# Strided attention's second product with V as the stationary operand, normalised by a ones matmul and Ln/Exp

## The chip, the cores and the metric

The kernel runs on one core of a Trainium2 chip. The metric is the device time of one execution in microseconds (us), lower is better; the median of several executions is given. A profile is one further execution recorded by the hardware profiler. The core has five engines that run their own instruction queues in order: TensorE (PE in the profile, PEld for its weight loads), VectorE (DVE), ScalarE (ACT), GpSimd (POOL) and SyncE (SP), the last used for DMA issue. Matmuls write to PSUM, which VectorE and ScalarE read.

## What is computed

A sparse attention over 8 batches and 8 heads (sequence 576, head dimension 64), followed by a two-layer network with squared relu over the 4608 tokens:

```python
pos = np.arange(S)
rel = pos[:, None] - pos[None, :]
mask_local = (rel >= 0) & (rel < 32)
mask_strided = (rel >= 0) & (pos[None, :] % 32 == pos[:, None] % 32)
masks = np.stack([mask_local if h < H // 2 else mask_strided for h in range(H)])
scores = np.where(masks[None], scale * (q @ k.T), -1e9)      # per batch and head
attn = softmax(scores)
x = (attn @ v).transpose(0, 2, 1, 3).reshape(B * S, H * D)   # 4608 x 512
h = np.maximum(x @ w_in, 0.0)                                # 4608 x 2048
out = (h * h) @ w_out                                        # 4608 x 512, float32
```

Heads 0 to 3 of a batch use the local mask, heads 4 to 7 the strided one. Under the strided mask a query sees only keys of its own residue modulo 32.

## The kernel before

Attention is done in 32 units, four per batch: unit u is batch u // 4 and head pair u % 4. Pairs 0 and 1 are local, 2 and 3 strided. The kernel holds x transposed in four tiles `xt[p]` (128 rows are the two heads' 64 features, 4608 columns are tokens), because the first layer of the network reads x with features on the partitions.

For a strided unit the 576 positions of a head are split into 8 blocks of 72 (`SP_`) positions: 4 residues with their 18 members each. A score block is 72 by 72 and needs a mask that is the same for all blocks.

The steps of a unit, each a function:

- `step_T` (L256): transposes q and k on TensorE, in the first batches only; later they come from transposing DMAs.
- `step_S` (L291): score matmuls (L314), 16 for a strided unit, with keys on the output's partitions, so that the exponentials `e` have keys on partitions and queries in the columns. The exponential runs on ScalarE (L319, four of 288 columns), the mask is a multiply on VectorE (L325). `e` is one of four standing tiles.
- `step_D` (L395): the second product. `e` is the stationary operand and V the moving one; V's tile has a 65th column of ones, so that the sum of a row of `e` comes out beside its products (L412). A strided unit has 16 such matmuls in three parts of 6, 6 and 4 (one PSUM tile each). VectorE takes the reciprocal of the sums (L426) and multiplies (L427) into a tile x with queries on the partitions.
- `step_E` (L430): brings x into `xt`: for local units of batch 2 and later by a transposing DMA, for strided units by 8 transposes on TensorE (L444) and a copy out of PSUM with reordered columns (L452, on ScalarE for units below 12, on VectorE from then on).

Batch 0 goes another way, written out by hand in `first_steps` (L516): `step_N` (L354) multiplies a tile of ones (128 by 64) with `e`, which gives the row sums replicated on 64 partitions (L361); ScalarE takes Ln (L363) and Exp with scale -1 (L364) of them, which is the reciprocal; `step_O` (L366) uses V as the stationary operand and `e` as the moving one (L380), which gives x transposed, and VectorE multiplies the two into `xt` (L391).

The network works on 9 chunks of 512 tokens. A group of the first layer is four 512-wide matmuls (L468) into a `ph` PSUM tile (two buffers), a relu on ScalarE (L474) and a square on VectorE (L475). A group of the second layer is four 512-wide matmuls (L486); every fourth group ends with a copy on ScalarE (L497) and a store. Chunk 2's first layer stands alone; from chunk 3 on groups of chunk c's first layer alternate with groups of chunk c-1's second layer into a single `py` buffer.

The order is static. A planner gives each group of the network a due number: how many attention steps have been emitted before it. Each batch's steps are spread by weight over the groups that precede the chunk which first reads that batch, and end two groups ahead of it. `stream_steps` (L558) writes the order of steps: for each u, S of unit u+1, E of unit u-1, then the parts of D of unit u. `later(n, fn, key)` defers an engine instruction by n groups, and `run_due` at the head of a step emits what its unit still has pending. PSUM tiles `pt` of all steps come from one pool of five (`ps_t`).

Of the kernel before, what the change touches and what calls it, by code (L numbers as in the profile page):

```python
# [8 lines left out]
FP32 = mybir.dt.float32  # L9
BF16 = mybir.dt.bfloat16  # L10
AF = mybir.ActivationFunctionType
ALU = mybir.AluOpType

@with_exitstack
def kernel(
# [9 lines left out]
    nc = tc.nc  # L25
    B, H, S, D = q.shape
# [4 lines left out]
    scale = 1.0 / (D ** 0.5)  # L31
    QL = 96
    NL = S // QL
    NJ = 8
    RH = STRIDE // NJ
    SP_ = RH * NA
# [7 lines left out]
    v_st = ctx.enter_context(tc.tile_pool(name="v_st", bufs=2))  # L44
    small = ctx.enter_context(tc.tile_pool(name="small", bufs=4))
    xl_pool = ctx.enter_context(tc.tile_pool(name="xl_pool", bufs=4))
    x_pool = ctx.enter_context(tc.tile_pool(name="x_pool", bufs=2))
    g_pool = ctx.enter_context(tc.tile_pool(name="g_pool", bufs=2))
    r_pool = ctx.enter_context(tc.tile_pool(name="r_pool", bufs=4))
    y_pool = ctx.enter_context(tc.tile_pool(name="y_pool", bufs=4))  # L50

    PS = bass.MemoryType.PSUM
# [4 lines left out]
    ps_t = ctx.enter_context(tc.tile_pool(name="ps_t", bufs=5, space=PS))  # L57
# [12 lines left out]
    xt = [singles.tile([128, T], BF16, name=f"xt{p}") for p in range(4)]  # L70
# [3 lines left out]
    ones = singles.tile([128, D], BF16)  # L74
# [17 lines left out]
    units = [(b, p) for b in range(B) for p in range(H // 2)]  # L92
    st = {}

    def is_local(u):
        return units[u][1] < H // 4
# [145 lines left out]
    def later(n, fn, key=None):  # L242
        pending.append((clock[0] + n, key, fn))

    def run_due(test):
        due = [x for x in pending if test(x)]
        for x in due:
            pending.remove(x)
        for x in sorted(due, key=lambda x: x[0]):
            x[2]()  # L250
# [5 lines left out]
    def step_T(u, name):  # L256
        s = st[u]
        local = is_local(u)
        n, w = (6, QL) if local else (NJ, SP_)
        src = s[name]  # L260
        if u != 1:
            src = src.rearrange("p j h d -> p (j h d)" if local else "p h c -> p (h c)")
        pt = ps_t.tile([128, S], BF16, name="pt")
        for j in range(n):
            if u == 1:
                for h in range(2):
                    nc.tensor.transpose(pt[64 * h:64 * h + 64, w * j:w * (j + 1)],
                                        src[:, h, D * j:D * (j + 1)], ident[0:w, 0:w])
            else:
                nc.tensor.transpose(pt[:, w * j:w * (j + 1)], src[:, 128 * j:128 * (j + 1)],  # L270
                                    ident[0:w, 0:w])
        if local and name == "k":
            full = kTl[v_slot(u)]
            dst = full[:, 32:32 + S]
        else:
            full = dst = qkT.tile([128, S], BF16, name=f"{name}T")
        if local:
            o = dst.rearrange("c (p j) -> c p j", j=6)
            i = pt.rearrange("c (j p) -> c p j", j=6)
        else:  # L280
            o, i = dst, pt
        if name == "q" and u not in (1, 2, 3):
            nc.scalar.copy(o, i)
        else:
            nc.vector.tensor_copy(o, i)  # L285
        s[name + "T"] = full

    def blk_pos(h, j):
        return NJ * (j % 2) + 4 * h + j // 2
# [64 lines left out]
    def step_N(u):  # L354
# [8 lines left out]
            nc.scalar.activation(rv0[:, u, hw * half:hw * (half + 1)], pn[:, 0:hw], AF.Ln)  # L363
        nc.scalar.activation(rv0[:, u], rv0[:, u], AF.Exp, scale=-1.0)  # L364

    def step_O(u):  # L366
        s = st.pop(u)
        e, local, i = s["e"], is_local(u), u % 2
        kn, w, hw = (128, QL, S // 2) if local else (SP_, SP_, S // 2)
        pos = []  # L370
        for half in range(2):
            po = ps_t.tile([128, 512], FP32, name="pt")
            for t in range(hw // w):
                for h in range(2):
                    if local:
                        tt = NL // 2 * half + t
                        vt, c = vl0[:, i, h, tt], S * h + w * tt
                    else:
                        vt, c = vs0[:, i, NJ * h + 2 * t + half], S * half + hw * h + w * t
                    nc.tensor.matmul(po[64 * h:64 * h + 64, w * t:w * (t + 1)], vt, e[0:kn, c:c + w],  # L380
                                     start=True, stop=True)
            pos.append(po)

        def scaled():
            for half, po in enumerate(pos):
                cols = slice(hw * half, hw * (half + 1))
                o, x, r = xt[u][:, cols], po[:, 0:hw], rv0[:, u, cols]
                if not local:
                    o = xt[u][:, 0:S].rearrange("c (p j r) -> c p j r", j=NJ // 2, r=2)[:, :, :, half]
                    x, r = (y.rearrange("c (j p) -> c p j", p=SP_) for y in (x, r))  # L390
                nc.vector.tensor_tensor(o, x, r, op=ALU.mult)  # L391

        return scaled

    def step_D(u, part):  # L395
        run_due(lambda x: x[1] == u)
        s = st[u]
        e, vt = s["e"], s["v"]
        if is_local(u):
            w, kn, n0, n1, tot = QL, 128, 6 * part, 6 * part + 6, 2 * NL  # L400
            rhs = vt.rearrange("p h t d -> p (h t) d")
            pos = lambda n: QL * n
            src = lambda n: n
        else:
            w, kn, tot = SP_, SP_, NBS
            n0, n1 = ((0, 6), (6, 12), (12, 16))[part]
            rhs = vt
            pos = lambda n: SP_ * blk_pos(n % 2, n // 2)
            src = lambda n: NJ * (n % 2) + n // 2
        po = ps_t.tile([128, 6, D + 1], FP32, name="pt")  # L410
        for n in range(n0, n1):
            nc.tensor.matmul(po[:, n - n0, :], e[0:kn, pos(n):pos(n) + 128],  # L412
                             rhs[0:kn, src(n), 0:D + 1], start=True, stop=True)
        if part == 0:
            if is_local(u):
                s["x"] = xl_pool.tile([w, tot, D], BF16, name="x_l")
            else:
                s["x"] = x_pool.tile([w, tot, D], BF16, name="x_s")
        x = s["x"]
        if is_local(u):  # L420
            x = x.rearrange("p (t h) d -> p h t d", h=2)[:, part]
        else:
            x = x[:, n0:n1, :]
        m = n1 - n0
        rinv = small.tile([128, 6, 1], FP32, name="rinv")
        nc.vector.reciprocal(rinv[0:w, 0:m], po[0:w, 0:m, D:D + 1])  # L426
        nc.vector.tensor_tensor(x, po[0:w, 0:m, 0:D],  # L427
                                rinv[0:w, 0:m].to_broadcast([w, m, D]), op=ALU.mult)
# [71 lines left out]
    T_ = lambda u, nm: (lambda: step_T(u, nm))  # L500
    S_ = lambda u: (lambda: step_S(u))
    D_ = lambda u, part: (lambda: step_D(u, part))
    E_ = lambda u: (lambda: step_E(u))

# [11 lines left out]
    def first_steps():  # L516
# [11 lines left out]
        def outs(u):  # L528
            scaled[u] = step_O(u)
# [25 lines left out]
    def has_T(u):  # L555
        return units[u][0] < (LB if is_local(u) else XB)

    def stream_steps(lo, hi, base):  # L558
        order = [T_(lo, "q"), T_(lo, "k"), T_(lo + 1, "q"), S_(lo), T_(lo + 1, "k")]
        ends = {}  # L560
        for u in range(lo, hi + 1):
            if u < hi - 1:
                order.append(S_(u + 1))
            ahead = u + 2 < hi and has_T(u + 2)
            if ahead:
                order.append(T_(u + 2, "q"))
            if u > lo:
                order.append(E_(u - 1))
                ends[u - 1] = base + len(order)
            if u < hi:  # L570
                order.append(D_(u, 0))
                if ahead:
                    order.append(T_(u + 2, "k"))
                order.append(D_(u, 1))
                if not is_local(u):
                    order.append(D_(u, 2))
        return order, ends
# [95 lines left out]

    NCH = T // 512
    steps, ends = stream_steps(4, 8, 0)
    more, more_ends = stream_steps(8, 4 * B, len(steps))
    steps = steps + more
    ends.update(more_ends)
# [112 lines left out]
```

## Time and profile before

| | us |
|---|---|
| median of 6 runs | 316.88 (316.37 to 318.46) |
| the profiled execution, whole time | 317.12 |
| its span, first to last instruction | 315.1 |
| VectorE busy | 172.0 |
| ScalarE busy | 162.7 |
| POOL busy | 89.0 |
| L468, first layer: 572 matmuls recorded | 145.0 |
| L486, second layer: 576 matmuls | 145.5 |
| L412, second product of attention: 392 matmuls | 22.9 |
| L444, transposes of x: 124 matmuls | 7.4 |

How to read it: a busy time is the union of the recorded durations of an engine's instructions. A matmul's recorded duration contains its way through the array, so consecutive matmuls overlap in the records, and the time that a block of them takes from TensorE is read from the starts. The difference of about 2 us between an execution's whole time and its span lies before the first and after the last instruction.

### The profile page before, as it was taken

The page shows a single profiled execution, that of the slowest core. Times are in us where ns is not written, and L with a number is a line of the kernel's source. Part 1 is how long each engine was busy: PE and PEld are TensorE (multiplying, and loading weights), DVE is VectorE, ACT ScalarE, POOL GpSimd, SP SyncE. Part 2 cuts the span into 40 slices and gives each one's busy share as a digit, 9 for nine tenths or more (in the row PEclk, how much of TensorE's full clock was granted, in tenths as well). Part 3 has the DMA queues.
Part 4 walks back from the last instruction along what each step waited for, and adds up shares of the span by engine and source line. Part 5 has one row for each costly group of instructions (what it writes and reads, how often), then busy time and mean ns, then how long its engine had stood idle before and what let it go on. Part 6 is the DMA issues. An engine that isn't in the chain of part 4 may idle for free.

```text
span 315.1 us, 6213 instructions
## 1 busy us (share of the span) xinstructions
PE 303.8 (96%) x2384; PEld 149.4 (47%) x2384; DVE 172.0 (55%) x415; ACT 162.7 (52%) x337; POOL 89.0 (28%) x117
## 2 busy tenths in 40 slices
PE   8899989899999999999999999999999999999994
PEld 3444555444555444444444444444454444444441
DVE  6765655469876885576479646564454222222200
ACT  3846746477455765555555555555533434344311
POOL 8518843707830704281066025000000000000000
PEclk9969999999999999999999999999999999999999
DMA  8999999999999999999899795002111000000111
GB/s 146 163 207 204 206 188 258 213 257 221 190 163 202 211 200 192 183 247 214 157 229 204 151 207 88 23 30 60 57 47 41 34 35 34 33 35 33 63 70 67
DMA packets 89404, 43.81 MB, mean 139 GB/s; under 512 B 74112, under 2 KB 82976, under 8 KB 89184
## 3 DMA queue, kind: packets, MB, share of 16 engines
q1 hardware_dynamic: 74352, 32.91, 48.6%
q0 software_dynamic: 14880, 10.39, 22.9%
q8 instruction: 18, 0.29, 0.4%
q14 instruction: 10, 0.08, 0.1%
q10 hardware_dynamic: 144, 0.13, 0.1%
HBM read 36.70 MB, written 12.98 MB: 158 GB/s over the span
## 4 chain that ended last, share of the span: by engine, by line
PE 86%; DVE 7%; ACT 3%; DMA 1%; issue 1%; DVEq 0%
PE ph L468 38%; PE py L486 27%; PE ph L486 10%; PE pt L314 3%; PE pt L412 3%; DVE e L325 2%; DVE x_s L427 2%; PE pt L270 2%; PE pt L444 1%; DVE g_sb L475 1%; ACT e L319 1%; DMA q_st<-in_q_dram 1%; ACT r L474 1%; PE py L511 1%; DVE kTl L285 1%
## 5 line engine op out<-in xcount | busy, mean ns | idle before, releaser
L468 PE MATMUL ph<-xt,w_in_b 128*128 128x512 bf16 x572 | 145.0, 382 | 0.3 <-ACT r L474 0.3
L474 ACT ACTIVATE r<-ph 128x512 bf16<-128x512 f32 x143 | 85.3, 597 | 99.8 <-PE ph L468 98.2
L475 DVE TENSOR_TENSOR g_sb<-r 128x512 bf16<-128x512 bf16 x144 | 71.4, 501 | 101.3 <-ACT r L474 100.7
L486 PE MATMUL py<-w_out_b,g_sb 128*128 128x512 bf16 x400 | 102.7, 379 | 0.0
L486 PEld LDWEIGHTS <-g_sb 128*128 128x128 bf16 x576 | 52.7, 98 | 56.5
L468 PEld LDWEIGHTS <-w_in_b 128*128 128x128 bf16 x576 | 52.0, 98 | 55.3 <-issue 2.4
L319 ACT ACTIVATE e<-pt 128x288 bf16<-128x288 f32 (+1 forms) x128 | 47.3, 407 | 12.6 <-PE pt L314 12.4
L486 PE MATMUL ph<-w_out_b,g_sb 128*128 128x512 bf16 x176 | 42.8, 379 | 0.0
L412 PEld LDWEIGHTS <-e 128*128 128x128 bf16 (+1 forms) x392 | 20.8, 97 | 16.0 <-DVE e L325 0.6
L192 POOL CAST vl<-vl_st 128x768 bf16<-128x768 f32 x12 | 11.0, 914 | 53.3 <-DMA vl_st<-in_v_dram 53.1
L427 DVE TENSOR_TENSOR x_s<-pt,rinv 72x384 bf16<-72x384 f32 (+1 forms) x42 | 21.4, 509 | 1.4
L123 POOL CAST q_l<-q_st 96x768 bf16<-96x768 f32 x14 | 12.3, 882 | 25.3 <-DMA q_st<-in_q_dram 16.3
L325 DVE TENSOR_TENSOR e<-e,mask_loc 128x576 bf16<-128x576 bf16 x32 | 17.5, 546 | 2.2 <-ACT e L319 2.2
L325 DVE TENSOR_TENSOR e<-e,mask_str 72x576 bf16<-72x576 bf16 x32 | 17.6, 554 | 1.8 <-ACT e L319 1.8
L426 DVE RECIPROCAL rinv<-pt 96x6 f32<-96x6 f32 (+2 forms) x70 | 12.9, 184 | 8.4 <-PE pt L412 8.4
L497 ACT COPY y<-py 128x512 f32<-128x512 f32 x25 | 14.6, 585 | 4.4 <-PE py L486 4.1
L427 DVE TENSOR_TENSOR x_l<-pt,rinv 96x384 bf16<-96x384 f32 x28 | 15.5, 554 | 1.0
L123 POOL CAST k_l<-k_st 96x768 bf16<-96x768 f32 x14 | 12.7, 910 | 10.9 <-DMA k_st<-in_k_dram 10.7
L497 ACT COPY y<-ph 128x512 f32<-128x512 f32 x10 | 5.8, 585 | 17.4 <-PE ph L486 17.4
L208 POOL CAST vs<-v_st 72x1024 bf16<-72x1024 f32 x12 | 13.1, 1118 | 0.4
L412 PE MATMUL pt<-vs,e 72*128 72x65 bf16 x224 | 13.1, 193 | 0.0
L511 PE MATMUL py<-y 128*128 128x512 bf16 x24 | 9.9, 503 | 1.3 <-DVE y L637 1.3
(87 smaller groups left out, 166.7 us busy)
## 6 DMA issues: line engine op xcount, KB each, us to landing
out_dram<-y SPq DMA_DIRECT2D x35, 256.0 KB, 2.0
vl_st<-in_v_dram SPq DMA_DIRECT2D x24, 144.0 KB, 4.5
v_st<-in_v_dram SPq DMA_DIRECT2D x12, 288.0 KB
q_st<-in_q_dram SPq DMA_DIRECT2D x16, 144.0 KB, 4.7
k_st<-in_k_dram SPq DMA_DIRECT2D x16, 144.0 KB, 6.1
w_in_b<-in_moe_w_in_dram POOLq DMA_DIRECT2D x4, 512.0 KB, 12.6
w_out_b<-in_moe_w_out_dram POOLq DMA_DIRECT2D x4, 512.0 KB, 10.8
q_st<-in_q_dram SPq DMA_DIRECT2D x7, 288.0 KB, 9.9
```

Of the source, the lines that this page charges most:

```text
L123: copy(t.rearrange("p j h d -> p h j d"), s[name + "f"].rearrange("p h (j d) -> p h j d", j=6))
L208: (copy or nc.gpsimd.tensor_copy)(t[:, :, 0:D], s["vf"].rearrange("p h (j d) -> p (h j) d", d=D))
L319: nc.scalar.activation(e[0:kn, lo:lo + S // 2], banks[row][half][0:kn, 0:S // 2], AF.Exp, scale=scale)
L325: nc.vector.tensor_tensor(x, x, m.to_broadcast([kn, n, w]), op=ALU.mult)
L412: nc.tensor.matmul(po[:, n - n0, :], e[0:kn, pos(n):pos(n) + 128], rhs[0:kn, src(n), 0:D + 1], start=True, stop=True)
L427: nc.vector.tensor_tensor(x, po[0:w, 0:m, 0:D], rinv[0:w, 0:m].to_broadcast([w, m, D]), op=ALU.mult)
L468: nc.tensor.matmul(ph, w_in_b[:, kk, 128 * ff:128 * (ff + 1)], xt[kk][:, 512 * c:512 * (c + 1)], start=(kk == order[0]), stop=(kk == order ...
L474: nc.scalar.activation(r, ph, AF.Relu)
L475: later(1, lambda: nc.vector.tensor_tensor(g[:, ff, :], r, r, op=ALU.mult))
L486: nc.tensor.matmul(py, g[:, ff, 128 * j:128 * (j + 1)], w_out_b[:, ff, :], start=(ff == 0), stop=(ff == 15))
L497: nc.scalar.copy(y, py)
L511: nc.tensor.matmul(pw, idle_w[:, 0:128], idle_w[:, 0:512], start=True, stop=True)
```

## The change

From batch 3 on (units 14, 15, 18, 19 and so on to 30, 31: ten units) the strided units no longer run `step_D` and `step_E`. In place of `step_D` they run `step_R`, which does what `step_N` does in batch 0: four ones matmuls of 288 columns, two Ln, one Exp. In place of `step_E` they run `step_Q`, which does what `step_O` does in batch 0: sixteen matmuls with V as the stationary operand, and two multiplies on VectorE straight into `xt`. The second Ln, the Exp and the second multiply are deferred by one, two and one groups. The result of Ln and Exp, 128 by 576 in f32, lies in a new pool `rv_pool` of two buffers, from which the x tiles of the earlier strided units are now cut as well (the pool `x_pool` is gone). Each of these units makes two steps where it made four, so the planner spreads the steps of batches 3 to 7 anew. Local units and batches 0 to 2 keep their steps.

```diff
-    x_pool = ctx.enter_context(tc.tile_pool(name="x_pool", bufs=2))
+    rv_pool = ctx.enter_context(tc.tile_pool(name="rv_pool", bufs=2))
...
+    XO = 3
+
+    def by_cols(u):
+        return not is_local(u) and units[u][0] >= XO
+
+    def step_R(u):
+        run_due(lambda x: x[1] == u)
+        s = st[u]
+        e, hw = s["e"], S // 2
+        s["r"] = r = rv_pool.tile([128, S], FP32, name="rv")
+        for half in range(2):
+            pn = ps_t.tile([128, 512], FP32, name="pt")
+            for h in range(2):
+                c = S * half + hw * h
+                nc.tensor.matmul(pn[64 * h:64 * h + 64, 0:hw], ones[0:SP_], e[0:SP_, c:c + hw],
+                                 start=True, stop=True)
+            ln = lambda half=half, pn=pn: nc.scalar.activation(r[:, hw * half:hw * (half + 1)], pn[:, 0:hw], AF.Ln)
+            if half == 0:
+                ln()
+            else:
+                later(1, ln, u)
+        later(2, lambda: nc.scalar.activation(r, r, AF.Exp, scale=-1.0), u)
+
+    def step_Q(u):
+        run_due(lambda x: x[1] == u)
+        s = st.pop(u)
+        b, p = units[u]
+        e, vt, r, hw = s["e"], s["v"], s["r"], S // 2
+        for half in range(2):
+            po = ps_t.tile([128, 512], FP32, name="pt")
+            for t in range(hw // SP_):
+                for h in range(2):
+                    c = S * half + hw * h + SP_ * t
+                    nc.tensor.matmul(po[64 * h:64 * h + 64, SP_ * t:SP_ * (t + 1)],
+                                     vt[:, NJ * h + 2 * t + half, 0:D], e[0:SP_, c:c + SP_],
+                                     start=True, stop=True)
+            o = (xt[p][:, b * S:(b + 1) * S]
+                 .rearrange("c (p j r) -> c p j r", j=NJ // 2, r=2)[:, :, :, half])
+            mul = lambda o=o, po=po, half=half: nc.vector.tensor_tensor(
+                o, po[:, 0:hw].rearrange("c (j p) -> c p j", p=SP_),
+                r[:, hw * half:hw * (half + 1)].rearrange("c (j p) -> c p j", p=SP_), op=ALU.mult)
+            if half == 0:
+                mul()
+            else:
+                later(1, mul)
...
-                s["x"] = x_pool.tile([w, tot, D], BF16, name="x_s")
+                t = rv_pool.tile([128, S], FP32, name="rv").bitcast(BF16)[0:w, 0:tot * D]
+                s["x"] = t.rearrange("p (n d) -> p n d", d=D)
...
             if u > lo:
-                order.append(E_(u - 1))
+                order.append((lambda u=u - 1: step_Q(u)) if by_cols(u - 1) else E_(u - 1))
                 ends[u - 1] = base + len(order)
-            if u < hi:
+            if u < hi and by_cols(u):
+                order.append(lambda u=u: step_R(u))
+                if ahead:
+                    order.append(T_(u + 2, "k"))
+            elif u < hi:
                 order.append(D_(u, 0))
```

## The prediction, made before the changed kernel was run

> **What bounds the kernel now.** I read the page's busy shares first, then its forty slices, then the waits, and last the timeline of TensorE alone in the stretch that the change touches.
>
> ```profile
> span 315.1 us, 6213 instructions
> ...
> PE 303.8 (96%) x2384; PEld 149.4 (47%) x2384; DVE 172.0 (55%) x415; ACT 162.7 (52%) x337; POOL 89.0 (28%) x117
> ...
> PE   8899989899999999999999999999999999999994
> ...
> PEclk9969999999999999999999999999999999999999
> ```
>
> TensorE is at nine tenths in every slice from the tenth to the end and has its full clock there; VectorE and ScalarE are a little over half busy. One slice is 7.9 us. The strided units of batches 3 to 7 lie between about 98 and 240 us, so inside that solid row.
>
> ```profile
> DVE g_sb L475 <- ACT r L474: 100.7, 111, 3.1
> ACT r L474 <- PE ph L468: 98.2, 123, 4.0
> ```
>
> These are the two longest waits: VectorE waits for ScalarE, and ScalarE for TensorE. Nothing of comparable size waits the other way. Since a busy TensorE need not be a full one, I then read when each block of matmuls starts. Columns of the next two fences: start in us, length, engine, line, instruction, count. A block's price is the distance from its start to the next block's start, because the lengths overlap.
>
> ```profile
> 157.81 0.38 PE L468 MATMUL ph<-xt,w_in_b 128*128 128x512 bf16 x1
> 158.12 0.47 PE L314 MATMUL pt<-qT_s,kT_s 64*72 64x72 bf16 x16
> 158.52 1.04 PE L486 MATMUL py<-w_out_b,g_sb 128*128 128x512 bf16 x4
> 159.40 1.03 PE L468 MATMUL ph<-xt,w_in_b 128*128 128x512 bf16 x4
> 160.26 1.03 PE L486 MATMUL py<-w_out_b,g_sb 128*128 128x512 bf16 x4
> 161.12 0.35 PE L412 MATMUL pt<-vs,e 72*128 72x65 bf16 x6
> 161.31 1.03 PE L468 MATMUL ph<-xt,w_in_b 128*128 128x512 bf16 x4
> ...
> 164.95 0.29 PE L412 MATMUL pt<-vs,e 72*128 72x65 bf16 x4
> 165.07 1.03 PE L468 MATMUL ph<-xt,w_in_b 128*128 128x512 bf16 x4
> ...
> 168.99 0.42 PE L444 MATMUL pt<-ident,x_s 72*128 72x72 bf16 x8
> 169.25 1.03 PE L468 MATMUL ph<-xt,w_in_b 128*128 128x512 bf16 x4
> ```
>
> Every group of four wide matmuls takes 0.86 us (159.40 to 160.26), that is 0.216 each; no gap is left. So in this stretch the end moves by exactly what a block on TensorE gains or loses; time saved on VectorE buys nothing here.
>
> **What the Trainium skill says.** "TensorEngine Tiling (Array Packing)", Key Properties: a change of tiling mode drains the array. The trace agrees: the score block L314, which uses 64-row tiles, makes the wide matmul before it last 0.31 (157.81 to 158.12) or more where 0.216 is normal, and the group behind it takes 0.88 in place of 0.86; L412 and L444, which use the whole array, do neither. The same page, Restrictions, says that column tiling switches Fast Weight Load off: loads of 64 columns for L361 and L380 average 107 to 137 ns in the trace, those of 128 columns for L412 97, so half the columns are not quicker. "ScalarE: Activation LUTs", Table sets, puts Ln and Exp in one set, natural_log_exp_and_others; the trace has a single table load (1.3 us, at the start) although batch 0 runs both, so the new Ln and Exp cost no reload.
>
> **The change, part by part.** It concerns ten units (batches 3 to 7, pairs 2 and 3).
>
> Removed from TensorE, per unit: the three blocks of step D, 161.12 to 161.31 = 0.19, a second six the same 0.19, and four at 164.95 to 165.07 = 0.12; the eight transposes of step E, 168.99 to 169.25 = 0.26. Sum 0.76 us for 24 matmuls. All of it is on the path.
>
> Added to TensorE, per unit: step R, four 288-wide ones matmuls, and step Q, sixteen 72-wide ones with V as weights, both with outputs of 64 partitions, so in column tiles. Batch 0 already runs both shapes for its strided units (72 rows; 12.24 and 15.58 for R, 15.85 for Q), and the windows view gives a granted clock of 1.00 from 7.3 to 17.4 us:
>
> ```profile
> 11.92 0.39 PE L511 MATMUL py<-y 128*128 128x512 bf16 x1
> 12.24 0.44 PE L361 MATMUL ph<-e,ones 72*64 72x288 bf16 x4
> 12.61 0.39 PE L511 MATMUL py<-y 128*128 128x512 bf16 x1
> ...
> 15.26 0.39 PE L511 MATMUL py<-y 128*128 128x512 bf16 x1
> 15.58 0.44 PE L361 MATMUL ph<-e,ones 72*64 72x288 bf16 x4
> 15.85 0.43 PE L380 MATMUL pt<-e,g_sb 72*64 72x72 bf16 x16
> 16.21 0.39 PE L511 MATMUL py<-y 128*128 128x512 bf16 x1
> ```
>
> R between two full-array blocks: 12.24 to 12.61 = 0.37, and the wide matmul ahead of it takes 0.32 (11.92 to 12.24) where 0.216 is normal: 0.10 more. With R followed by another block of the same mode it is 0.27 (15.58 to 15.85), so leaving the mode costs another 0.10, which is already in the 0.37. Q, left for the full array: 15.85 to 16.21 = 0.36, exit included; entered from the full array it pays the same 0.10 as R. To each I add the 0.01 to 0.02 that the group behind L314 loses (taken 0.01). In the changed program's instruction order every one of the ten R and ten Q stands alone between groups of full-array matmuls, never next to the other or to a score block, so each pays both drains: R 0.48, Q 0.47, sum 0.95 us for 20 matmuls. Fewer instructions, but four changes of mode where there were none.
>
> Difference: 0.95 - 0.76 = 0.19 per unit, times ten = +1.9 us. Bounds: readings are to 0.01, some six per unit, and a Q whose weights strided by 72 load a little slower, or whose loads reach ahead a little better: 0.13 to 0.27 per unit, +1.3 to +2.7 us.
>
> VectorE, per unit: gone are three reciprocals (0.19, 0.19, 0.17), three multiplies (0.55, 0.55, 0.42) and the copy L452 (0.75): 2.82. New are two multiplies of 128x288 from PSUM, at L391's mean of 0.54: 1.08. Minus 17 us over ten units, on an engine that waits 100.7 us for ScalarE's relu: worth nothing to the end. The multiplies wait for Q and for R's Exp; behind them in VectorE's queue are the squares L475 and masks L325. Q follows its R by four groups or more and a score block; by three groups for unit 30 and two (1.73 us) for unit 31. Since the two Ln and the Exp, with the relu of one group between, are done about 3.1 us after R's start and unit 31's Q ends at about 2.6, only that multiply waits, some 0.6 us. The last strided unit of a batch has two groups, 1.73 us, before the first matmul that reads its x, against 0.2 + 2 x 0.54 = 1.3 us; that matmul takes this pair's x as its fourth operand, 0.65 later. No stall.
>
> ScalarE, per unit: two Ln of 128x288 (0.41 to 0.43 at L363) and one Exp of 128x576 in f32 (0.68 at L364): 1.5 us, plus 15 over all, to about 178 of 317. Hidden in its 98 us of waiting, if they do not fall in the wrong place. There are two such places. One is the stretch from about 100 to 117 us, where the first-layer groups stand without second-layer groups between: a relu of 0.60 is due every 0.86, with only two ph buffers, and the windows view shows ScalarE busy 13.2 of 18.0 us; both strided units of batch 3 land there and bring 3.0. The order puts R, two groups, scores, two groups, Q, so that TensorE's own small blocks (0.5 each) give the relu time: I take nothing, upper end 0.5 a unit. The other is the copy L497 out of the single py buffer: TensorE needs it back one group (0.86) after the matmuls end, and the copy takes 0.59. In the order of the changed program an Ln stands before such a copy (as an exponential of 0.40 does now, without a stall), an Exp never does. Cost nothing, upper end 0.25 each.
>
> Buffers: R takes two and Q two of the five pt, in place of D's three and E's one; rv has two buffers and R of one unit comes after Q of the one two before. POOL's casts into vs wait for Q instead of D's last block, some groups later, but POOL spends 53.1 us waiting for the v loads. No DMA is added or removed. The steps are spread anew because each of these units now makes two fewer; score blocks of later batches come a little later against their loads, not earlier.
>
> The sum stands against the profiled execution's own 317.12 us (span 315.1 and 2.0 around it): 319.0. That execution lies 0.24 above the median of 316.88, so the forecast for the median is 318.8 us.
>
> **Rivals.** (a) Faster: the drains are not paid. Place: the entry and exit of each R and Q. Were weights and matmuls of the two column halves to flow through, R would cost 0.27 and Q 0.26 (0.36 less its exit), 0.53 against 0.76, and ten units would give -2.3: 314.6. It speaks for it that batch 0's blocks stand among few neighbours in a stretch with short waits; against it that three different wide matmuls ahead of column-tiled blocks take 0.32, and L314 shows the same in the stretch in question. It decides from the point where a change of mode costs under 0.057 us (0.23 over four) in place of 0.105. (b) Slower by more: ScalarE takes TensorE's place in batch 3 and at the y copies: 2 x 0.5 and, say, three of 0.25 on top: 318.8 + 1.7 = 320.5. For it: a relu queue with 0.27 idle per group; against it: the order, as told. (c) No change: VectorE's relief ends small stalls elsewhere. TensorE's stalls on VectorE (L444 and L314 before 90 us) lie in batches 1 and 2, which keep the old path; what could be regained after 98 us is nil. That would need 1 to 2 us: about 317.
>
> **How the numbers follow.** The forecast 0.80, (a) 0.08, (b) 0.09, (c) 0.03. About 0.3% (0.95 us) is what can be told from no change: 315.9 to 317.8. The forecast's own range is 318.2 to 319.6; with its lower tail and part of (b) 317.5 to 320.5. Faster 0.07, same 0.08 (c, and the edges of the forecast and (a)), slower 0.85.
>
> **What would show it.** Right: ones blocks of 0.37 and V blocks of 0.36, start to start, each with a wide matmul of 0.32 ahead; 2344 matmuls; VectorE near 155 us, ScalarE near 178; no gap over 0.15 in TensorE past 100 us. Wrong: R and Q together under 0.76 with their edges (a); TensorE idle on ScalarE's relu or Exp, around 100 to 117 us or behind a y copy (b).

## The result and the profile after

| | before | changed |
|---|---|---|
| median, us | 316.37 (63 runs) | 318.68 (28 runs) |
| profiled execution, whole time and span | 317.12, 315.1 | 318.73, 317.0 |
| VectorE busy | 172.0 | 154.4 |
| ScalarE busy | 162.7 | 174.3 |
| start of unit 14's scores | 93.6 | 92.3 |
| from there to the group behind the last attention block | 146.5 | 149.7 |

The ratio is 1.0074, with a 95% interval from 1.0056 to 1.0093: 2.3 us slower, 1.8 to 2.9. The forecast was 318.8 us. In what follows a ones block is the four matmuls of `step_R` and a V block the sixteen of `step_Q`. Single executions of either kernel spread over 4 us and more, so the experiments below are read from medians with their intervals and, more sharply, from the starts in the traces. Of one run, b0_before_again, only the times are used, since its trace was taken in an execution of 323.18 us at a TensorE clock of 0.948.

The page of the changed kernel, the lines shown of before:

```profile
span 317.0 us, 6118 instructions
...
PE 303.7 (96%) x2344; PEld 144.1 (45%) x2344; DVE 154.4 (49%) x365; ACT 174.3 (55%) x367; POOL 89.5 (28%) x117
...
PE   7889989999999999999999999999999999999994
...
PEclk9979999999999999999999999999999999999999
```

TensorE has 40 matmuls fewer and the same 96%; the digits show nothing of the loss. The longest waits and one new one, from the view of waits (us in total, times, longest):

```profile
DVE g_sb L522 <- ACT r L521: 117.0, 111, 3.0
ACT r L521 <- PE ph L515: 89.0, 113, 2.4
...
PE pt L314 <- DMA kTl<-k_l: 1.2, 1, 1.2
```

VectorE's 17.6 us of relief have gone into its waiting for the relu, 100.7 us before and 117.0 now. The third line is new: TensorE waits for transposed keys. The timeline of TensorE in batch 5 of the changed kernel (start, length, line, instruction, count):

```profile
164.50 1.03 PE L533 MATMUL py<-w_out_b,g_sb 128*128 128x512 bf16 x4
165.37 1.03 PE L515 MATMUL ph<-xt,w_in_b 128*128 128x512 bf16 x4
166.32 0.44 PE L380 MATMUL pt<-e,ones 72*64 72x288 bf16 x4
166.69 1.04 PE L533 MATMUL py<-w_out_b,g_sb 128*128 128x512 bf16 x4
...
170.62 1.03 PE L533 MATMUL py<-w_out_b,g_sb 128*128 128x512 bf16 x4
171.58 0.45 PE L399 MATMUL pt<-e,vs 72*64 72x72 bf16 x16
171.96 1.04 PE L515 MATMUL ph<-xt,w_in_b 128*128 128x512 bf16 x4
172.84 1.03 PE L533 MATMUL py<-w_out_b,g_sb 128*128 128x512 bf16 x4
```

A plain group takes 0.87 (164.50 to 165.37, read to 0.01). The group ahead of the ones block takes 0.95 (165.37 to 166.32) and the one ahead of the V block 0.96; the blocks take 0.37 and 0.38; the group behind takes 0.88. So a unit costs 0.37 + 0.38 + 2 x 0.09 + 2 x 0.01 = 0.95 to 0.96 us where it was 0.75 to 0.76, and ten units 2.0 us.

The weight loads (PEld) show what is missing at a change of mode. The first four lines are of before, the last three of the changed kernel; the brackets hold the loader's idle time and what ended it ("issue": nothing that the profile shows):

```profile
144.06 0.28 PEld L314 LDWEIGHTS <-kTl 64*128 64x128 bf16 x12 [0.42 <-issue]
144.07 0.43 PE L314 MATMUL pt<-kT,kTl 64*128 64x96 bf16 x12
...
145.09 0.51 PEld L444 LDWEIGHTS <-x_s 72*128 72x128 bf16 x8
145.30 0.42 PE L444 MATMUL pt<-ident,x_s 72*128 72x72 bf16 x8
...
108.10 0.14 PEld L380 LDWEIGHTS <-ones 72*64 72x64 bf16 x4 [0.42 <-DVE g_sb L522]
108.10 0.44 PE L380 MATMUL pt<-e,ones 72*64 72x288 bf16 x4
108.46 1.41 PEld L515 LDWEIGHTS <-w_in_b 128*128 128x128 bf16 x8 [0.23 <-issue]
```

The transposes L444 stay in the mode of the full array: their first weights load from 145.09, while the last wide matmul still runs, 0.21 us ahead of their first matmul. At the ones block the loader stands idle for 0.42 us and begins together with the matmuls, and behind the block it is the same: the wide group loads from 108.46 and starts at 108.47. All ten ones blocks show the 0.42 us, whatever is named as releaser. The scores L314 of a local unit show them too, and they load 128 columns of weights, so it is not the 64 columns that keep the load back.

The other part of the trace is one wait in batch 3, in the timeline of all engines (SPq is SyncE's issue of a DMA; in brackets idle time and what ended it):

```profile
105.68 1.33 SPq L173 DMA_TRANSPOSE kTl<-k_l  x1
...
108.10 0.44 PE L380 MATMUL pt<-e,ones 72*64 72x288 bf16 x4
...
108.47 1.90 PE L515 MATMUL ph<-xt,w_in_b 128*128 128x512 bf16 x8
...
111.55 0.43 PE L314 MATMUL pt<-kT,kTl 64*128 64x96 bf16 x12 [1.18 <-DMA kTl<-k_l]
```

The scores of unit 17 (the second local unit of batch 4) wait 1.18 us for keys whose transposing DMA was issued at 105.68. Between the two profiles, then: 1.3 us less up to unit 14's scores, where both kernels run the same steps (TensorE had half its clock there for 6.8 us in before's profile and for 3.4 in the changed kernel's), 2.0 us more for changes of tile mode, and 1.2 us more for this wait; together the 1.9 us between the spans.

### The profile page after: what moved, and what is told of

It is laid out like the page before. It is cut to its first block, busy times and chain, and to the rows that moved or that the text cites. A ratio compares the mean times of both kernels' runs of the same rounds, so it can differ in the third digit from the quotient of the medians.

```text
span 317.0 us, 6118 instructions
## 1 busy us (share of the span) xinstructions
PE 303.7 (96%) x2344; PEld 144.1 (45%) x2344; DVE 154.4 (49%) x365; ACT 174.3 (55%) x367; POOL 89.5 (28%) x117
## 4 chain that ended last, share of the span: by engine, by line
PE 83%; DVE 6%; DMA 5%; POOL 3%; ACT 1%; issue 1%; POOLq 0%; DVEq 0%
PE ph L515 37%; PE py L533 27%; PE ph L533 10%; PE pt L314 3%; DMA g_sb<-in_v_dram 3%; DMA kTl<-k_l 2%; DVE rv L474 2%; PE pt L458 2%; DVE e L325 1%; PE pt L270 1%; PE pt L399 1%; PE pt L380 1%; DVE g_sb L522 1%; ACT r L521 1%; DVE kTl L285 1%
## 5 line engine op out<-in xcount | busy, mean ns | idle before, releaser
L522 DVE TENSOR_TENSOR g_sb<-r 128x512 bf16<-128x512 bf16 x144 | 66.8, 465 | 117.8 <-ACT r L521 117.0
L319 ACT ACTIVATE e<-pt 128x288 bf16<-128x288 f32 (+1 forms) x128 | 48.0, 407 | 11.9 <-PE pt L314 11.8
L325 DVE TENSOR_TENSOR e<-e,mask_str 72x576 bf16<-72x576 bf16 x32 | 18.8, 591 | 7.9 <-ACT e L319 7.8
L325 DVE TENSOR_TENSOR e<-e,mask_loc 128x576 bf16<-128x576 bf16 x32 | 17.5, 547 | 3.7 <-ACT e L319 3.7
L458 PEld LDWEIGHTS <-e 128*128 128x128 bf16 (+1 forms) x232 | 12.0, 97 | 9.1 <-DVE e L325 0.8
L208 POOL CAST vs<-v_st 72x1024 bf16<-72x1024 f32 x12 | 14.1, 1204 | 0.4
L404 DVE TENSOR_TENSOR xt<-pt,rv 128x288 bf16<-128x288 f32 x20 | 12.1, 638 | 0.7 <-ACT rv L387 0.6
L458 PE MATMUL pt<-vl,e 128*128 128x65 bf16 x168 | 9.9, 193 | 0.7 <-DVE e L325 0.7
L473 DVE RECIPROCAL rinv<-pt 96x6 f32<-96x6 f32 (+2 forms) x40 | 7.4, 185 | 6.2 <-PE pt L458 6.2
L558 PE MATMUL py<-y 128*128 128x512 bf16 x24 | 9.0, 462 | 1.3 <-DVE y L688 1.3
```

The costliest lines, as they stand in the source:

```text
L208: (copy or nc.gpsimd.tensor_copy)(t[:, :, 0:D], s["vf"].rearrange("p h (j d) -> p (h j) d", d=D))
L319: nc.scalar.activation(e[0:kn, lo:lo + S // 2], banks[row][half][0:kn, 0:S // 2], AF.Exp, scale=scale)
L325: nc.vector.tensor_tensor(x, x, m.to_broadcast([kn, n, w]), op=ALU.mult)
L404: mul = lambda o=o, po=po, half=half: nc.vector.tensor_tensor(o, po[:, 0:hw].rearrange("c (j p) -> c p j", p=SP_), r[:, hw * half:hw * (ha ...
L522: later(1, lambda: nc.vector.tensor_tensor(g[:, ff, :], r, r, op=ALU.mult))
```

## The experiments

The ratios below are to executions of the kernel before made beside each run (medians 316.07 to 316.29 us). "Drain theory" in the recorded expectations is the prediction's account: each entry into column tiles and each exit from them costs TensorE about 0.1 us.

The sharpest measure is the stretch from the scores of unit 18 to those of unit 31, which holds six of the ten units (batches 4 to 6). The two starts are read from each trace, and 0.863 us for each group of four wide matmuls between them is taken off (in before's trace three groups take 2.59, from 113.74 to 116.33); the rest is what attention costs TensorE there, waits included. The groups are counted from the weight loads. Some traces lack a few per cent of the matmul records; such a place shows as three matmuls where four are issued, with 0.16 us of idle, and is no wait. Each row is one trace.

| run | the two starts, us | groups between | rest, us | entries into column tiles |
|---|---|---|---|---|
| before | 119.38, 222.63 | 104 | 13.5 | 0 |
| changed | 121.50, 228.54 | 107 | 14.7 | 12 |
| e0_after_again | 120.59, 227.63 | 107 | 14.7 | 12 |
| e1_merge_q_r | 123.48, 230.51 | 107 | 14.7, of it 0.7 a wait | 9 |
| e2_split_q | 123.81, 232.20 | 107 | 16.0 | 18 |
| e3_same_spacing | 118.48, 222.93 | 104 | 14.7 | 12 |
| e4_act_load | 118.78, 222.03 | 104 | 13.5 | 0 |
| e5_merge_same_spacing | 120.81, 224.58 | 104 | 14.0 | 9 |
| e7_two_blocks | 118.55, 223.17 | 104 | 14.9, of it 1.5 waits | 6 |

**e0_after_again**: the changed kernel, unedited.

> The changed kernel once more, beside the runs below. The drain theory (ten units, each with two changes into and two out of column tiles, 0.10 us each, against 0.23 us saved on the matmuls themselves) expects 2.0 us more than before, 1.0065, and in the trace 0.37 and 0.38 us for every ones and V block with a wide matmul of about 0.31 ahead. If the wait of unit 17's scores for its transposed keys (1.2 us at 110 us in the first profile) belongs to the change and not to that one execution, it is there again, and part of the loss is the new spacing of the steps.

319.48 us (6 runs), 1.0093 of before (1.0056 to 1.013). The blocks are as in the first profile, the rest is 14.7 again, and the wait of unit 17 is there again with 0.69 us. So the first profile was no exception on either point.

**e2_split_q**: each V block in two halves.

```diff
-        for half in range(2):
+
+        def one(half):
             po = ps_t.tile([128, 512], FP32, name="pt")
...
-            mul = lambda o=o, po=po, half=half: nc.vector.tensor_tensor(
+            nc.vector.tensor_tensor(
...
-            if half == 0:
-                mul()
-            else:
-                later(1, mul)
+
+        one(0)
+        later(1, lambda: one(1))
```

> The V block is cut into its two halves, the second emitted one group of wide matmuls later: same matmuls, ten exits and ten entries more. Drain theory: 10 x 0.2 = 2.0 us more than the changed kernel, 1.013 of before. Rivals (ScalarE's load, spacing of the steps): as the changed kernel, 1.007.

320.04 us, 1.0126 (1.0088 to 1.0164). Its timeline of TensorE:

```profile
180.22 1.03 PE L533 MATMUL py<-w_out_b,g_sb 128*128 128x512 bf16 x4
181.17 0.32 PE L400 MATMUL pt<-e,vs 72*64 72x72 bf16 x8
181.43 1.04 PE L515 MATMUL ph<-xt,w_in_b 128*128 128x512 bf16 x4
182.39 0.32 PE L400 MATMUL pt<-e,vs 72*64 72x72 bf16 x8
182.65 1.04 PE L533 MATMUL py<-w_out_b,g_sb 128*128 128x512 bf16 x4
```

Eight matmuls take 0.26, not half of the sixteen's 0.38, and the groups ahead take 0.95 and 0.96: both halves pay. The rest grew by 1.35 us for six entries more, 0.22 each. The matmuls, their operands and the work of the other engines are the same, so the price is in the change of mode.

**e1_merge_q_r**: the opposite direction, first try: the second unit's ones block straight behind the first unit's V block.

```diff
-                order.append((lambda u=u - 1: step_Q(u)) if by_cols(u - 1) else E_(u - 1))
+                if by_cols(u - 1) and u < hi and by_cols(u):
+                    order.append(lambda u=u: (step_Q(u - 1), step_R(u)))
+                else:
+                    order.append((lambda u=u - 1: step_Q(u)) if by_cols(u - 1) else E_(u - 1))
...
-                order.append(lambda u=u: step_R(u))
+                order.append((lambda: None) if by_cols(u - 1) else (lambda u=u: step_R(u)))
```

> The ones block of the second strided unit of each batch is put straight behind the V block of the first, with an empty step in its old place so that all other steps stay where they were. Same matmuls, five exits from and five entries into column tiles fewer. Drain theory: 5 x 0.2 = 1.0 us less than the changed kernel, 1.003 of before. Rival, ScalarE's new Ln and Exp or the instruction counts hold TensorE up: no difference to the changed kernel, since all of these stay, 1.007. Rival, spacing of the steps: no difference either.

319.34 us, 1.0087 (1.006 to 1.0114): no gain. The trace shows why the median doesn't fall. The merged block comes two groups after a score block and needs PSUM tiles that ScalarE's exponentials have not yet read: the ten ones blocks take 4.9 us, start to start, where they take 3.7 in the changed kernel (the 1.7 us that e5's expectation names come from 5.4, which counts two missing records as time). Two of the five merged blocks wait, 0.7 each, those of batches 3 and 4. And unit 17's wait was 1.89 us in this execution, after which the clock fell; the windows view (window and its length, busy time of PE, PEld, DVE, ACT and POOL with counts, then PEclk, DMA share and GB/s):

```profile
109.90:112.00 2.10, 0.21 (x3) 0.05 (x4) 0.88 (x3) 0.60 (x1) 0.43 (x1) 1.00 1.28 217
112.00:113.40 1.40, 1.40 (x17) 0.74 (x18) 0.00 (x0) 0.42 (x2) 0.00 (x0) 0.99 1.35 295
113.40:116.80 3.40, 3.18 (x23) 1.36 (x23) 2.02 (x5) 1.79 (x4) 0.00 (x0) 0.50 1.06 210
```

TensorE is nearly idle in the first row and has half its clock for the 3.4 us of the third. In the stretch of the table the one merged block that waits loses the 0.7 us that three entries fewer save: 14.7 less 0.7 is 14.0, which e5, without that wait, shows directly.

**e5_merge_same_spacing**: as e3 (below), with the V block moved back to the ones block instead of the reverse, so that it stands three groups or more behind the scores.

```diff
+                pair = by_cols(u - 1) and u < hi and by_cols(u)
+                order.append((lambda: None) if pair else
+                             (lambda u=u - 1: step_Q(u)) if by_cols(u - 1) else E_(u - 1))
...
+                order.extend([(lambda u=u: (step_Q(u - 1), step_R(u))) if by_cols(u - 1)
+                              else (lambda u=u: step_R(u)), lambda: None, lambda: None])
```

> As e3 (two empty steps for each strided unit, score blocks where the kernel before has them), and the V block of the first strided unit of a batch is put straight ahead of the ones block of the second, three groups or more after the scores, so that the PSUM tiles it needs are free. Drain theory: five entries and five exits fewer than e3, 1.0 us less, that is 1.0 us or 1.0032 over before, and in the trace no wait of the ones blocks for ScalarE (in e1 they lost 1.7 us so). Rivals: as e3, 1.0065.

318.34 us (6 runs), 1.0073 (1.0049 to 1.0098): the median alone doesn't show the microsecond. The trace does: the rest is 14.0 where e3 has 14.7, 0.7 us for three entries fewer, 0.23 each, and the ones blocks wait for nothing.

```profile
170.57 1.03 PE L515 MATMUL ph<-xt,w_in_b 128*128 128x512 bf16 x4
171.53 0.45 PE L399 MATMUL pt<-e,vs 72*64 72x72 bf16 x16
171.81 0.41 PE L380 MATMUL pt<-e,ones 72*64 72x288 bf16 x4
```

The V block that is followed by another block of its mode takes 0.28 (171.53 to 171.81) in place of 0.38, and the ones block pays no entry. In this execution unit 17 waited 1.21 us, more than the gain.

**e7_two_blocks**: as e3, with both ones blocks of a batch together and both V blocks together.

```diff
-                order.append((lambda u=u - 1: step_Q(u)) if by_cols(u - 1) else E_(u - 1))
+                order.append((lambda: None) if by_cols(u - 1) else E_(u - 1))
...
-                order.append(lambda u=u: step_R(u))
+                if by_cols(u - 1):
+                    order.extend([lambda u=u: (step_R(u - 1), step_R(u)), lambda: None,
+                                  lambda u=u: (step_Q(u - 1), step_Q(u))])
+                else:
+                    order.extend([lambda: None] * 3)
```

> As e3, but of each batch's two strided units the ones blocks stand together and the V blocks stand together, four groups later: two entries and two exits a batch in place of four (five in e1's manner). The traces so far put one entry with its exit at 0.2 to 0.23 us. Drain theory: between the scores of unit 18 and those of unit 31 TensorE's time outside the wide matmuls falls from 14.68 us (changed kernel) to 13.3 to 13.5, as low as before (13.48); median as before, 1.000 to 1.002. If the price sat in the matmuls themselves it would stay at 14.68.

317.81 us, 1.0047 (1.0024 to 1.007). The blocks came out as expected, the rest did not:

```profile
168.37 1.03 PE L515 MATMUL ph<-xt,w_in_b 128*128 128x512 bf16 x4
169.32 0.68 PE L380 MATMUL pt<-e,ones 72*64 72x288 bf16 x8
169.94 1.04 PE L533 MATMUL py<-w_out_b,g_sb 128*128 128x512 bf16 x4
...
175.97 0.34 PE L314 MATMUL pt<-kT,kTl 64*128 64x96 bf16 x7
176.50 0.28 PE L314 MATMUL pt<-kT,kTl 64*128 64x96 bf16 x5 [0.18 <-DVE xt L404]
```

Two ones blocks in one take 0.62 (169.32 to 169.94), not 2 x 0.37, and pay one entry. But two V blocks hold four of the five `pt` tiles until VectorE's multiplies have read them, and the scores two groups later wait for one: twelve score matmuls take 0.75 (175.97 to 176.72, where the next group starts) in place of 0.36. Over the three batches in the stretch these blocks lose 1.5 us beyond their 0.36. Without that the rest would be 13.4, what the drain theory expected (13.3 to 13.5) and no more than before has; that is a sum, not a run.

**e4_act_load**: the kernel before with ScalarE's load added.

```diff
+    def act_load():
+        one = lambda: nc.scalar.activation(fill, fill, AF.Exp, scale=0.0)
+        one()
+        later(1, one)
+        later(2, one)
+        later(2, one)
...
+        if part == 0 and not is_local(u) and units[u][0] >= 3:
+            act_load()
```

> The kernel before, with four activations of 128x288 added to ScalarE's queue at each strided unit of batches 3 to 7, deferred as the changed kernel's Ln and Exp are (1.6 us a unit; their result is not used). Drain theory: ScalarE has the room, no difference to before, 1.000. Rival, ScalarE's added work holds TensorE up: up to the 2.3 us of the change, 1.003 to 1.007.

317.07 us, 1.0029 (1.0006 to 1.0051). In the stretch of batches 4 to 6 the rest is 13.5, equal to before within a hundredth: ScalarE's added work costs nothing there. The excess sits ahead of it. The trace has TensorE waiting 1.1 us for the key transposes of units 16 and 17 and 0.5 for ScalarE's relu near 100 us, where first-layer groups stand alone. So ScalarE's load doesn't explain the changed kernel's loss in batches 4 to 6; in batch 3 it may add something, which this run does not separate from the transposes.

**e3_same_spacing**: two empty steps behind each ones block, so that the planner counts as before.

```diff
-                order.append(lambda u=u: step_R(u))
+                order.extend([lambda u=u: step_R(u), lambda: None, lambda: None])
```

> Two empty steps stand behind each ones block, so that a strided unit makes as many steps as before and every score block and every batch end is at the group where the kernel before has it. Drain theory: the 2.0 us stay, 1.0065 of before. Rival, the new spacing brings score blocks ahead of their key transposes: the wait of unit 17's scores goes, and 0.3 to 1.2 us of the loss with it, 1.003 to 1.0055.

318.64 us, 1.0077 (1.0049 to 1.0104), the rest 14.7: with the old spacing the mode changes cost what they cost in the new. Unit 17 did not wait in this trace, but the median is not lower than the changed kernel's by anything that can be told.

Is the wait of unit 17 a matter of the spacing? In the new spacing its scores come one group earlier (17 groups behind unit 14's, not 18). TensorE's wait for transposed keys ahead of the scores of units 16 and 17 was 1.18, 0.69, 1.89 and 2.17 us in the four traces with that spacing (changed, e0, e1, e2) and 0, 0.03, 1.08, 1.21, 0.54 and 0 in six with the old one (before, e3, e4, e5, e6, e7). So it can happen in either; in these traces it is in all four of the new and in three of six of the old.

**e8_transposes_earlier, e9_before_transposes_earlier, e10_two_blocks_earlier**: the transposes of local q and k four groups earlier in SyncE's queue, in the changed kernel, in the one before, and in e7.

```diff
-            at(g + 14 + 4 * i, lambda u=4 * b + i: transpose_local(u))
+            at(g + 10 + 4 * i, lambda u=4 * b + i: transpose_local(u))
```

> The changed kernel with the transposing DMAs of the local units' q and k (batches 4 to 7) put four groups earlier into SP's queue, ahead of the v loads. If the wait of unit 17's scores is for a transpose that stands too late in that queue, the stretch from unit 14's to unit 17's scores loses the 0.7 to 1.2 us seen in the two profiles of the changed kernel, and the median falls by as much, to about 1.005. If it is a matter of the score blocks' new places alone, this changes it too; if the DMA engines are simply full then, it stays.

> The kernel before with the same earlier transposes. If the wait belongs to the new spacing alone, nothing to gain, 1.000. If it can happen in the old spacing too (e4 and e5 showed 0.8 and 1.2 us of it), 0 to 0.8 us less than before, 0.9975 to 1.000.

> e7 and e8 together, the version meant to be no worse than before: drain theory and the earlier transposes together give 0.9975 to 1.001 of before. Rivals: as the changed kernel, 1.007.

320.98, 318.24 and 320.32 us; 1.0137 (1.0082 to 1.0191), 1.0065 (1.0043 to 1.0086) and 1.0146 (1.0095 to 1.0197). None of the three traces has a wait for transposed keys. For e8 that tells something, since all four earlier traces with its spacing have one: the place in the queue mattered. All three are slower all the same, by 2.2 to 2.5 us against their like. In e9 the order of instructions on TensorE, VectorE, ScalarE and POOL is that of before, but in batch 2 TensorE now waits for VectorE where it did not:

```profile
84.65 0.35 PE L412 MATMUL pt<-vs,e 72*128 72x65 bf16 x6
...
85.96 0.41 PE L270 MATMUL pt<-ident,k_l 96*128 96x96 bf16 x6 [0.96 <-DVE x_s L427]
...
88.45 0.29 PE L412 MATMUL pt<-vs,e 72*128 72x65 bf16 x4 [0.88 <-DVE x_s L427]
```

The transposes of keys and the last part of the second product wait for tiles that VectorE's multiplies still read; in before the same two follow without such a wait. Most of the loss lies behind this point: e9 and e4 have the same steps up to unit 14's scores and ran at full clock up to there; they are level at this place (84.65 and 84.56 us), and unit 14's scores start at 93.3 in e9, at 91.0 in e4. From unit 18 to 31 e9's rest is 13.6 and e8's 14.7, as without the move. Why a moved DMA brings these waits stayed open; another assignment of PSUM tiles is a guess that no run tested. As a remedy the move failed.

**e6_batches_1_2_only**: the new path where VectorE did hold TensorE up.

```diff
-        return not is_local(u) and units[u][0] >= XO
+        return not is_local(u) and 1 <= units[u][0] < XO
```

> The new path for the strided units of batches 1 and 2 only, the old one from batch 3 on. There the profile of before has TensorE waiting for VectorE's multiplies (about 0.9 us at each of two transposes, 54.9 and 58.3 us). Drain theory: four units x 0.2 = 0.8 us more on TensorE, and these two waits of 0.9 go: 1.0 us less than before, 0.997. Rival, the waits only move to the Ln and Exp, or the relief of VectorE is worth nothing here either: 0.8 us more than before or worse, 1.0025.

318.73 us (6 runs), 1.0107 (1.0068 to 1.0145): slower by 3.4 us, more than the 0.8 us of mode changes. The two waits of transposes on the strided multiplies are gone, but the ones blocks now wait for masks (0.8 us) and score blocks for exponentials (0.9) and for the key copies on VectorE (1.9 in four waits, up to 92 us): the wait moved, as the rival had it. The rest from unit 18 to 31 is 13.5, as it must be.

**b0_before_again**: the kernel before, unedited.

> The kernel before once more, for its trace beside the others of this call: from the first strided scores of batch 3 to the last attention block it should again take 146.5 us with no wait of TensorE, whatever its first 93 us take. If those first 93 us come out 1 to 2 us shorter this time, the difference seen there between the two first profiles is chance; if they come out at 93.6 again, the changed kernel gains something there.

316.38 us, 1.0006 (0.9989 to 1.0024). For the first 93 us the other traces answer: unit 14's scores start at 93.6 (before), 92.3 (changed), 91.9 (e0), 91.0 (e4) and 91.3 (e3), all with the same steps up to there. The changed kernel's 1.3 us there are chance: the time at half clock in the first 25 us was 6.8 us in before's profile, 3.4 in changed and e3, none in e0 and e4. The stretch of 146.5 us could not be compared, since this trace had a lower clock throughout.

No version beat the kernel before. The best of the new path was e7 with 1.0047.

## Why the prediction was right

The direction, the size and the mechanism came out as forecast. That 318.8 us lies within 0.2 of the median is in part luck: the forecast added 1.9 us to a median of 316.88 from six executions, which 63 executions put at 316.37, and the measured difference is 2.3. The 2.3 lies in the forecast's range of +1.3 to +2.7, and the part of it that the traces show on TensorE, 2.0, is close to the 1.9.

- **What bounds the kernel.** That only TensorE's starts count held: 17.6 us less on VectorE bought nothing, 11.6 more on ScalarE cost nothing in batches 4 to 6.
- **The sum.** R was put at 0.37 and is 0.37; Q at 0.36 and is 0.38; the entry at 0.10 and is 0.09; the group behind at 0.01 and is 0.01; removed was put at 0.76 and is 0.75. Forecast +1.9 us, on TensorE +2.0. The exit was read from batch 0 as 0.10, and e5 shows it: 0.28 against 0.38. The Trainium skill's sentence that a change of tiling mode drains the array ("TensorEngine Tiling (Array Packing)", Key Properties) agrees with every trace here, with 0.2 us or a little more for one entry and its exit, from three doses (e2, e5 and the changed kernel itself). The traces show the late weight loads on both sides of a block; what TensorE does inside these 0.2 us they don't show.
- **Rival (a), drains not paid**, is refuted by e2 and e5.
- **Rival (b), ScalarE as the bound.** At the copies out of `py` nothing happened. In the changed kernel no relu held TensorE up past 100 us. Small waits on it near 100 us do appear in e3, e4 and e5 (0.3 to 0.5), so the worry named the right place. The one wait of a multiply for its Exp that was forecast, 0.6 us for unit 31, is there with 0.59.
- **Rival (c)**: no stall went elsewhere, and e6 shows that in batches 1 and 2 VectorE's relief moves the stalls and doesn't end them.
- **One step was wrong**: "score blocks of later batches come a little later against their loads, not earlier", and with it "no gap over 0.15 in TensorE past 100 us". Counted in groups, the scores of units 17, 21, 25 and 29 come one group earlier (those of the other units from 15 on one to five later), and unit 17's then wait for their transposed keys, 1.18 and 0.69 us in the two profiles of the changed kernel. The forecast survived because such a wait also occurs in the old spacing at times, and the medians hold only a part of the difference. Whether the 0.3 us between 2.0 and the measured 2.3 are its doing stays open: the interval of the ratio is wider than that, and e3, with the old spacing, loses as much.
- **Durations that were off without effect**: the multiply L404 takes 0.64 us, not 0.54, and ScalarE is busy 174 us, not 178. VectorE's 154 us against the forecast 155 are in part luck, since its squares, on which nothing was forecast, fell from 71.4 to 66.8 us.

## What to carry to other kernels

Where a matmul stream has no gaps, price a block of small matmuls by the distance from its start to the next block's, and count every entry into and exit from another tile mode as part of it: here 0.2 us for a pair, 0.4 a unit, where the small matmuls themselves became only about 0.2 shorter (an estimate: 0.95 less two pairs, against 0.75). If such blocks are to pay, put them side by side, and count first the PSUM tiles that this holds and who frees them. A step that is dropped from a planned order moves the others too: count each one's distance to the loads that it needs.

## What was unexpected of the hardware

In e1 a wait of 1.89 us was followed by half the clock from 113.4 to 116.8 us. In e2 a wait of 1.63 us was not, so one trace suggests, and doesn't show, that a short stall can cost more than its length. In the first 25 us similar stretches come by chance: the trace of before has half clock from 17.5 to 24.3 us, that of e0 none, with nothing changed there.

At a change of tile mode the first weights of the next block are not loaded ahead. In the changed kernel's trace, past 93 us, they begin within 0.01 us of their matmul at all 37 entries and all 37 exits (ones blocks, V blocks and scores, of which only the rows are tiled). Ahead of the 18 blocks that stay in the full array's mode they begin 0.21 us earlier than their matmul.
